# An adaLN transformer block on one core: transfers in the order of need, planned to land later, with a freed residual load and reset stage knobs

## The chip, the core and the metric

The kernel runs on one core of a Trainium2 chip. A core has five engines, each with an instruction queue of its own: PE (TensorE, matmuls into PSUM), DVE (VectorE), ACT (ScalarE), POOL (GpSimd) and SP (SyncE, which here issues nearly all DMA transfers). The engines meet only at semaphores, and each works its instructions strictly in the order in which they were written. The metric is the device time of one execution in microseconds (us).

## The reference

One sequence of 2048 tokens with 640 features, 32 heads of 20, a bilinear gated unit of width 1536, all in bf16:

```
mod = silu(c) @ w_mod                      # six rows of 640: sa, ca, ga, sb, cb, gb
h   = layernorm(x) * (1 + ca) + sa
q, k, v = heads of (h @ wqkv)
p   = softmax(q k^T / sqrt(20))
x   = x + ga * ((p v) @ wo)
h   = layernorm(x) * (1 + cb) + sb
x   = x + gb * (((h @ w_gate) * (h @ w_up)) @ w_down)
```

## The kernel before

**Work and tiles.** The queries are cut into six chunks (512, 512, and four of 256), the heads into eight sets of four. One chunk with one set is an *item*; the very last is split in two, which makes 49. Within an item the scores of 128 keys by the chunk's queries are computed for four heads side by side on PE (line 1494). Two ways lead from scores to exponentials. Most go in groups of two PSUM banks to ACT (816 ACTIVATE instructions of 128x1024, line 1531). A fixed share (QUADS) goes to DVE, which moves them out of PSUM with a shift (line 1555) and builds the power of two from the bits of an int16 (lines 1587, 1595, 1592; a part of the products on POOL, line 1607). Then PE multiplies either kind with the values (line 2154) into the item's accumulator, whose first column is the sum of the softmax.

**Around the attention.** At the start x is loaded, normed and transposed, and Q, K and V are projected. Most of K and Q goes out to DRAM in packed rows and comes back set by set in the layout that the scores need (line 1250 writes from the buffers KPA and KPB, line 1263 loads KT, line 1272 loads QT); the projection of later sets runs beside the scores of earlier ones. At the end of an item DVE transposes the accumulator (T1, line 1686), takes the reciprocal (1691), POOL multiplies (1693), DVE transposes back into OcT (1702), and four or five transfers bring the rows into Ocp (1714). When all eight sets of a chunk are there, the chunk's *suffix* follows beside the scores of the next chunk: load of the residual x (1771) and output projection (944, with evacuation 1793), norm (1810 to 1817, with an addition and a power on POOL, 1813 and 1815), transposes (1855), gate and up (weights loaded by line 1896 into three stg buffers), product into hprod (1928 or 1959), down projection and store (2024, 2033). The last chunk's suffix has nothing beside it. The last two chunks have sets of buffers of their own: for the last but one the residual buffer xckt, and a hprod that lies on the same bytes as xckb, the residual buffer of odd chunks.

**What sets the order.** A planner in the kernel file (class Sched) simulates the engines when the program is built. Each operation is a Task with a duration, a list of tasks it needs, and a priority (a lower number goes first). Whenever an engine is free in the simulation, it takes the first task by priority that is ready by then; `pick_pe` chooses for PE between scores, values and projections with a row of knobs, which STAGE resets from item to item (a missing entry goes back to the default). A transfer is done, in the simulation, when its bytes have passed at DMA_RATE and a latency is over (`finish_issue`, lines 225 to 245); a few early ones have a landing time written by hand. The order that comes out is written into the engines' queues, with a semaphore wait wherever a task needs another. So the plan's times never reach the chip, only its order: if a transfer lands later on the chip than in the plan, the engine that needs it stands, and all that is queued behind it on that engine stands too. Where PE has nothing ready and has been too little busy lately (FILL_MIN), the plan puts a filler, matmuls on the identity without a result (line 2487).

DVE scores of later items ride in the group of an earlier item's scores (`d_attach`), which then waits for the later item's QT and KT as well, if the plan believes them landed.

Of the kernel before, what the change touches and what calls it, by code (L numbers as in the profile page):

```python
# [17 lines left out]
PV_W = 216.0  # L18
# [3 lines left out]
DMA_RATE = 350.0  # L22
# [5 lines left out]
DMA_LAT = 1700.0  # L28
STEAL_END = 66197.894
# [6 lines left out]
class Task:  # L36
    __slots__ = ("head", "hval", "hknow", "eng", "dur", "lat", "deps", "emits", "ctr", "prio", "gate", "acq", "on_start", "slots",
                 "start", "done", "needed", "val", "know", "nleft", "ready", "users", "name", "mode", "seq", "rt", "sem",
                 "nbytes", "cond", "alt", "land", "lk", "dead", "key")

    def __init__(self, eng, dur, emits, deps=(), ctr=None, prio=0.0, lat=None, gate=0, acq=(), on_start=None,
# [25 lines left out]
        self.land = 0.0  # L67
        self.lk = 0
# [58 lines left out]
class Sched:  # L127
# [213 lines left out]
def emit_program(nc, sched, nsem_dma=56):  # L341
# [130 lines left out]
PV_KEEP = 2  # L472
# [62 lines left out]
OPFIRST = 1500  # L535
HT_L = 0.25
# [10 lines left out]
    0: {"LKTOL": 300.0, "D_LATE": 16, "PVMIN": 2, "PVMAX": 14, "PVTOL": 249, "EAGER": 9, "XBACK": 0, "XDPRIO": 1.343, "X_HALF": 0.0, "HOLD": 95, "D_RES": 74, "STEAL_GAP": 200, "PVCAP": 12, "X_LATE": -179.96, "FILL_MIN": 4190.746, "TPRIO": 0.75, "PV_KEEP": 2},  # L547
    1: {"D_LATE": 17, "D_RES": 16, "EAGER": 3},
    2: {"DL": 0.376},
    3: {"PV_KEEP": 3, "HOLD": 128.0},  # L550
    4: {"HOLD": 131.9, "STEAL_GAP": 125.8},
    5: {"PVMAX": 4},
    6: {"PVTOL": 467.4, "X_LATE": -48.0, "D_LATE": 11},
    7: {"DL": 0.501},
    8: {"XBACK": 1},
    9: {"X_HALF": 75.1},
    11: {"DL": 0.443},
    12: {"DL": 0.459, "X_LATE": 52.1, "PVMAX": 4, "HOLD": 102.9},
    13: {"DL": 0.417},
    15: {"D_LATE": 17, "HOLD": 119.5},  # L560
    16: {"EAGER": 3, "X_HALF": 9.1, "HOLD": 111.6},
    19: {"DL": 0.471, "FILL_MIN": 2500, "LKTOL": 78.2},
    20: {"DL": 0.391, "HOLD": 136.1},
    24: {"DL": 0.464},
    25: {"DL": 0.549, "X_LATE": 54.0, "HOLD": 135.1},
    26: {"DL": 0.411, "X_LATE": 24.0, "D_LATE": 14},
    27: {"DL": 0.473, "X_LATE": 150.4, "PVCAP": 10, "HOLD": 149.2},
    29: {"X_HALF": -37.1, "PVMAX": 12, "HOLD": 127.7},
    30: {"X_LATE": -109.9, "HOLD": 140.4},
    31: {"X_HALF": 38.3, "X_LATE": 202.7, "D_RES": 21},  # L570
# [1992 lines left out]
```

## Time and profile before

| | us |
|---|---|
| median of 3 runs | 823.6 (822.26 to 826.3) |
| the profiled execution | 821.17 |
| its span in the profile | 819.4 |
| PE / ACT / DVE / POOL busy | 794.0 / 769.2 / 686.0 / 350.1 |
| granted TensorE clock, mean | 0.995 |

The span reaches from the first to the last instruction of the program; the time of the execution has 1.8 us more around it. The profile's tables by stage give the busy time of an engine in each stretch of the span, then the clock that was granted to TensorE (1.00 is full), the share of the 16 DMA engines in use and the GB/s they moved. The lists of waits say which instruction stood for whom; a wait for several things is put down to the one that came last by the profile, and where the engine named had long been done, it was another, often a transfer. In the list of DMA issues a time is that of the issuing on SP's queue, not of the movement.

### The profile page before, as it was taken

Reading aid. Unit: us, or ns where it says so; the run is one execution under the profiler, and the core shown is the slowest. Engines: PE = TensorE matmul, PEld = TensorE weight load, DVE = VectorE, ACT = ScalarE, POOL = GpSimd, SP = SyncE. Lnnn points to the kernel's source line nnn. Section 1 sums busy time; section 2 is a strip of 40 time slices with the busy share of each in tenths; the row PEclk is TensorE's granted clock in tenths of the full one; section 3 lists DMA queues with packets and bytes.
Section 4 is the critical chain, followed back from the end, with each engine's and each line's share of the span. In section 5 each row is a group of like instructions: output and inputs, shape, how many; then the busy total and the mean of one; then the engine's idle time right before and its main releaser. Section 6 shows DMA issues by size and latency. Waiting matters only on the chain.

```text
span 819.4 us, 34126 instructions
## 1 busy us (share of the span) xinstructions
PE 794.0 (97%) x14871; PEld 346.1 (42%) x14871; DVE 686.0 (84%) x1338; ACT 769.2 (94%) x853; POOL 350.1 (43%) x362
## 2 busy tenths in 40 slices
PE   8999999999989999999999999999999999999998
PEld 4433424332223322233344444444454555434667
DVE  7978887889979899899979878887699989798654
ACT  6899999999989999999999999999999999999931
POOL 3345535474645333244362534533463546035200
PEclk9999999999999999999999999999999999999999
DMA  9743112212340522103100222100441045441420
GB/s 301 233 117 90 49 52 69 58 34 76 99 117 12 155 65 53 45 3 90 35 9 7 56 69 63 36 23 22 96 101 39 26 99 117 107 101 39 97 66 26
DMA packets 136388, 60.49 MB, mean 74 GB/s; under 512 B 100704, under 2 KB 136240, under 8 KB 136240
## 3 DMA queue, kind: packets, MB, share of 16 engines
q1 hardware_dynamic: 135311, 57.16, 27.3%
q8 instruction: 118, 1.93, 1.0%
q10 hardware_dynamic: 928, 1.15, 0.4%
q14 instruction: 31, 0.25, 0.1%
HBM read 46.70 MB, written 8.99 MB: 68 GB/s over the span
## 4 chain that ended last, share of the span: by engine, by line
PE 55%; ACT 26%; DVE 11%; issue 4%; DMA 3%; SPq 1%; POOL 0%; DVEq 0%; ACTq 0%
ACT PP L1531 26%; PE ps_all L1494 18%; PE ps_all L944 18%; PE ps_all L2154 13%; DVE DB L1555 3%; PE ps_all L940 3%; DMA x<-in_A_x_dram 2%; PE ps_all L1204 2%; DVE DSS L1595 1%; DVE DSS L1587 1%; DVE st L1045 1%; DVE DSS L1592 1%; SPq L1714 1%; DMA stg<-in_B_w_up_dram 0%; DVE hT L1109 0%
## 5 line engine op out<-in xcount | busy, mean ns | idle before, releaser
L1531 ACT ACTIVATE PP<-ps_all 128x1024 bf16<-128x1024 f32 x816 | 753.1, 1086 | 10.2 <-PE ps_all L1494 9.4
L1607 POOL TENSOR_TENSOR DSS<-DB,DSS 128x512 bf16<-128x512 bf16 x248 | 281.9, 1158 | 320.0 <-DVE DSS L1595 259.8
L1494 PE MATMUL ps_all<-QT,KT 32*128 32x256 bf16 (+2 forms) x3136 | 321.6, 308 | 12.4 <-ACT PP L1531 9.0
L1555 DVE TENSOR_SCALAR DB<-ps_all 128x512 int16<-128x512 f32 x416 | 277.9, 684 | 60.4 <-PE ps_all L1494 58.4
L1494 PEld LDWEIGHTS ps_all<-QT,KT 32*128 32x128 bf16 x3136 | 89.6, 92 | 239.7 <-ACT PP L1531 183.5
L2154 PE MATMUL ps_all<-PP,Vf 128*32 128x256 bf16 (+2 forms) x2520 | 166.9, 311 | 0.0
L944 PE MATMUL ps_all<-h2T,stg 128*32 128x256 bf16 (+2 forms) x2260 | 124.7, 306 | 1.7 <-DMA stg<-in_B_w_up_dram 1.2
L2154 PE MATMUL ps_all<-DSS,Vf 128*32 128x256 bf16 (+1 forms) x1232 | 85.6, 315 | 0.5 <-DVE DSS L1592 0.3
L2154 PEld LDWEIGHTS ps_all<-PP,Vf 128*32 128x32 bf16 (+1 forms) x2520 | 49.8, 94 | 82.1 <-issue 76.4
L1595 DVE TENSOR_SCALAR DSS<-DB 128x2048 int16<-128x2048 int16 x104 | 74.1, 713 | 0.0
L1587 DVE TENSOR_SCALAR DSS<-DB 128x2048 int16<-128x2048 int16 x104 | 71.3, 685 | 0.3
L1693 POOL TENSOR_TENSOR OTn<-OT,invT 128x256 bf16<-128x256 f32 (+1 forms) x47 | 39.0, 830 | 66.1 <-DVE invT L1691 65.8
L944 PEld LDWEIGHTS ps_all<-h2T,stg 128*32 128x32 bf16 x2260 | 52.1, 96 | 30.2 <-issue 19.2
L944 PE MATMUL ps_all<-wd,hprod 128*32 128x320 bf16 (+1 forms) x1328 | 61.6, 283 | 0.0
L1592 DVE TENSOR_TENSOR DSS<-DB,DSS 128x2048 bf16<-128x2048 bf16 x42 | 52.5, 1251 | 0.2
L2154 PEld LDWEIGHTS ps_all<-DSS,Vf 128*32 128x32 bf16 (+1 forms) x1232 | 29.6, 95 | 21.8 <-issue 11.7
L944 PE MATMUL ps_all<-wV,hT 128*32 128x160 bf16 x1280 | 37.2, 234 | 0.4
L944 PEld LDWEIGHTS ps_all<-wd,hprod 128*32 128x32 bf16 x1328 | 30.0, 96 | 16.0 <-issue 10.4
L944 PE MATMUL ps_all<-wo,Ocp 128*32 128x320 bf16 (+1 forms) x692 | 30.5, 278 | 4.1 <-DMA Ocp<-OcT 3.0
L1686 DVE STREAM_TRANSPOSE OT<-ps_all 128x256 f32<-128x256 f32 (+2 forms) x49 | 25.7, 525 | 10.1 <-PE ps_all L2154 9.9
L1204 PE MATMUL ps_all<-hT,wk 128*32 128x512 bf16 (+1 forms) x360 | 31.8, 382 | 0.2
L1204 PE MATMUL ps_all<-hT,wq 128*32 128x512 bf16 x375 | 31.6, 382 | 0.1
(132 smaller groups left out, 526.7 us busy)
## 6 DMA issues: line engine op xcount, KB each, us to landing
stg<-in_B_w_gate_dram SPq DMA_DIRECT2D x62, 160.0 KB
stg<-in_B_w_up_dram SPq DMA_DIRECT2D x62, 160.0 KB
KT<-k_rows SPq DMA_DIRECT2D x112, 32.0 KB
wm<-in_w_mod_dram SPq DMA_DIRECT2D x3, 800.0 KB
x<-in_A_x_dram SPq DMA_DIRECT2D x7, 320.0 KB
k_rows<-KPA SPq DMA_DIRECT2D x16, 128.0 KB
QT<-q_rows SPq DMA_DIRECT2D x32, 64.0 KB
wd<-in_B_w_down_dram SPq DMA_DIRECT2D x1, 1920.0 KB
```

Source lines behind the costliest of these rows:

```text
L944: return lambda e, b: e.matmul(ps[32 * x:32 * x + 32, b, c0 + o:c0 + o + w], lhs()[:, 32 * x:32 * x + 32], rhs() if w == n else rhs()[:, o ...
L1204: f = [lambda e, b_, k=k, x=x: e.matmul(ps[x:x + min(32, w - x), b_, :], wx[:, k, r0 + x:r0 + min(x + 32, w)], hT[tc][:, k, :], tile_posit ...
L1494: ems.append(lambda e, i=i, kt=kt: e.matmul(dstf()[:, i * u.n:(i + 1) * u.n], KT[32 * u.s:32 * u.s + 32, u.j, kt * 128:(kt + 1) * 128], QT ...
L1531: return e.activation(PPs[g % 2][:, cellp["p"], 0:nu * 512], ps[:, b0:b0 + nu, :].rearrange("p b c -> p (b c)"), AFT.Exp, scale=ESCALE)
L1555: return e.tensor_scalar(DBl[st_["slot"]][:, x * 512:(x + 1) * 512], bank(cell["b"]), EBIAS, 0.0, op0=ALU.add, op1=ALU.max)
L1587: return e.tensor_scalar(DSl[st_["ss"][0]][:, :], DBl[st_["slot"]][:, :], 0x7F, 0x3F00, op0=ALU.bitwise_and, op1=ALU.bitwise_or)
L1592: return e.tensor_tensor(d, DBl[st_["slot"]][:, :].bitcast(BF16), d, ALU.mult)
L1595: return e.tensor_scalar(DSl[st_["ss"][1]][:, :], DBl[st_["slot"]][:, :], 0x7F80, 2, op0=ALU.bitwise_and, op1=ALU.bitwise_or)
L1607: return e.tensor_tensor(d, DBl[st_["slot"]][:, x * w:x * w + w].bitcast(BF16), d, ALU.mult)
L1686: t1 = Task("dve", n * 1.1 + 70, lambda e: e.transpose(OT[:, 0:n], ps[:, item_info[it]["bank"], 0:n].rearrange("p (b q r) -> p b r q", q=3 ...
L1693: f3 = lambda e: e.tensor_tensor(OTn[:, 0:n].rearrange("p (b c r) -> p b r c", c=32, r=2), OT[:, 0:n].rearrange("p (b r c) -> p b r c", c= ...
L2154: ems.append(lambda e, i=i, kt=kt, stt=stt, stp=stp: e.matmul(ps[32 * s:32 * s + mc, bk, 0:u.n], Vf[:, (kt * H + 4 * u.j + s) * VW:(kt * H ...
```

## The change

Five things are changed. (1) The planner's model: transfers after 25 us move at 240 GB/s instead of 350, and those issued after 60 us land 1000 ns later, unless marked `firm`; some matmul costs go up by 1 to 3 ns. (2) The priorities of transfers on SP's queue: writes of K and early Q rows, loads of KT and QT by set and chunk, and the pieces of Ocp of the last two sets. (3) In the suffix of the last but one chunk the residual load, the norm's output and the transposes no longer wait for the stores of xckb; hprod's writers do (`hp_free`). (4) At the end of a chunk the reciprocal and the second transpose have priority 0.4 instead of 1.5 on DVE, and the addition and power of the norm -1 instead of 1 on POOL. (5) The STAGE table is reset; its entry for item 0 and the DL values stay.

```diff
-PV_W = 216.0
+PV_W = 219.0
...
+DMA_RATE_2 = 240.0
+DMA_MARGIN = 1000.0
+DMA_M0 = 60000.0
...
-            self.dma_free = b + task.nbytes / DMA_RATE
-            task.done = task.land or self.dma_free + (DMA_LAT_2 if early else DMA_LAT + DMA_SLOW * task.nbytes)
+            self.dma_free = b + task.nbytes / (DMA_RATE if early or task.firm else DMA_RATE_2)
+            task.done = task.land or self.dma_free + (DMA_LAT_2 if early else DMA_LAT + DMA_SLOW * task.nbytes +
+                                                      (0.0 if task.firm or start < DMA_M0 else DMA_MARGIN))
...
+ENDP, END3, P_POW = 0.4, 0, -1.0
...
 STAGE = {
...
-    1: {"D_LATE": 17, "D_RES": 16, "EAGER": 3},
-    2: {"DL": 0.376},
-    3: {"PV_KEEP": 3, "HOLD": 128.0},
...
+    1: {"FILL_MIN": 4712.6, "PV_KEEP": 2, "LKTOL": 200.7},
+    2: {"DL": 0.376, "PVMAX": 4},
+    3: {"HOLD": 124.6},
...
-    43: {"HOLD": 179.1},
-    44: {"PV_KEEP": 1, "X_LATE": 6.7, "HOLD": 113.2},
-    45: {"HOLD": 117.9},
+    42: {"HOLD": 47.1, "XBACK": 0},
+    45: {"EAGER": 9, "PVTOL": 185.1},
 }
...
-    C512, C320, C128, C1 = 216.0, 136.0, 57.0, 26.0
+    C512, C320, C128, C1 = 219.0, 137.0, 57.0, 26.0
...
-        return max(n / 2.4 + 3.0, 60.0)
+        return max(n / 2.4 + 6.0, 60.0)
...
-                dst(), buf[p0:p0 + n_, cell["t"].slots["kp"], :]), [te], prio=1.5, dur=450.0)
+                dst(), buf[p0:p0 + n_, cell["t"].slots["kp"], :]), [te], prio=1.5 if late_q else 1.0, dur=480.0)
...
-                        dps, prio=1.4, dur=450.0) for s in range(4)]
+                        dps, prio=1.1 + .01 * (j + tc / 4), dur=480.0) for s in range(4)]
...
-                            [...], prio=1.6, dur=450.0)]
+                            [...], prio=1.11 + .01 * (j + NSET * ci), dur=480.0)]
...
+        pe_ = ENDP if j == NSET - 1 and ci < NC - 1 else 1.5
...
-                                            OT[:, 0:n].rearrange("p (b c) -> p b c", c=32)[:, :, 0:1]), [t1], prio=1.5)
+                                            OT[:, 0:n].rearrange("p (b c) -> p b c", c=32)[:, :, 0:1]), [t1], prio=pe_)
...
-            t = dma("sp", nr * n * 2, f, dps, prio=2, dur=720.0)
+            t = dma("sp", nr * n * 2, f, dps, prio=1.05 if j >= NSET - 2 else 2, dur=720.0)
+            t.firm = ci == NC - 1 and it >= len(items) - 2
...
-            first = list(sfx_done["qd1"]) + outs_r[1] if ci == NC - 2 else bd["tr"] + bd["h2T"] + bd["hp"] + outs_r[0]
+            first = list(sfx_done["qd1"]) if ci == NC - 2 else bd["tr"] + bd["h2T"] + bd["hp"] + outs_r[0]
+        hp_free = first + (outs_r[1] if ci == NC - 2 else [])
...
-            p1 = dve(75, f1, [ag], prio=LN2T if tail else LN2P) if tail else pool(220, f1, [ag], prio=1)
+            p1 = dve(75, f1, [ag], prio=LN2T if tail else LN2P) if tail else pool(220, f1, [ag], prio=P_POW)
...
-                      [p1], prio=1)
+                      [p1], prio=P_POW)
...
-                    return [eg, dve(ps_cost(n), f, [r.last, eg] + (first if alt else bd.get("hp", []) + proj_early + kv_last), prio=1)]
+                    return [eg, dve(ps_cost(n), f, [r.last, eg] + (hp_free if alt else bd.get("hp", []) + proj_early + kv_last), prio=1)]
```

More of the change, by code (lines that the diff above doesn't have):

```diff
@@ L67, in __init__ @@
         self.land = 0.0
+        self.firm = False
         self.lk = 0
@@ L568 @@
[L568 to L578 removed]
+    25: {"DL": 0.549},
@@ new lines @@
+    26: {"DL": 0.411, "X_LATE": 65.8, "PVMAX": 3, "EAGER": 8},
+    27: {"DL": 0.473},
+    29: {"HOLD": 38.5, "PVMIN": 2, "LKTOL": 11.4},
+    30: {"D_RES": 7, "PVMAX": 4, "X_HALF": -29.6},
+    31: {"X_LATE": -186.8, "X_HALF": 32.8, "HOLD": 130.6},
+    32: {"EAGER": 5, "D_LATE": 14, "HOLD": 153.7, "LKTOL": 269.4},
+    33: {"DL": 0.442, "XBACK": 4, "PV_KEEP": 1},
+    34: {"X_LATE": 5.0},
+    35: {"X_LATE": 15.7},
+    36: {"DL": 0.524, "EAGER": 3},
+    38: {"HOLD": 43.6},
+    42: {"HOLD": 47.1, "XBACK": 0},
@@ L1273, in packed_round @@
                             QT[ci][:, j, :], QS[1024 * tc + 128 * j:1024 * tc + 128 * j + 128, so:so + n]),
-                            [x for l in done for x in l] + q_zero[tc] + (x0_done if ci else []), prio=1.6, dur=450.0)]
+                            [x for l in done for x in l] + q_zero[tc] + (x0_done if ci else []), prio=1.11 + .01 * (j + NSET * ci), dur=480.0)]
             if tc not in LATEQ:
@@ L1697, in item_end_tasks @@
         direct = j == NSET - 1 and ci == NC - 1
-        if T3_POOL and not direct:
+        if T3_POOL and not direct and not (END3 and j == NSET - 1):
             t3 = pool(n * 2.2 + 200, f3, [t2], prio=0)
         else:
-            t3 = dvl(sb_cost(n, 1.04), f3, [t2], prio=1.5)
+            t3 = dvl(sb_cost(n, 1.04), f3, [t2], prio=pe_)
         t4 = dve(n * .55 + 65, lambda e: e.transpose(OcT[:, cell["s"], 0:n].bitcast(F32), OTn[:, 0:n].bitcast(F32)), [t3],
-                 prio=1.5)
+                 prio=pe_)
         pcs = [] if direct else oc_pieces(j)
```

40 lines of the change are left out of this document (17 added, 23 removed).

## The prediction

> **What bounds the kernel now.** I read the page first (busy shares, costliest groups), then the table by stage for the exponentials alone, then the waits of those stages in which that table shows a hole, then the chain and the DMA queue around each hole.
>
> ```profile
> PE 794.0 (97%) x14871; PEld 346.1 (42%) x14871; DVE 686.0 (84%) x1338; ACT 769.2 (94%) x853; POOL 350.1 (43%) x362
> L1531 ACT ACTIVATE PP<-ps_all 128x1024 bf16<-128x1024 f32 x816 | 753.1, 1086 | 10.2 <-PE ps_all L1494 9.4
> ```
>
> ACT carries 816 exponentials, 753.1 us of its 769.2, and stood idle before them for only 10.2 us in the whole run. PE shows 97%, but a busy PE is partly one that is paced by the exponentials. Which of the two sets the time is read by stage (columns: length, ACT busy with the exponentials and their count, granted clock, DMA share, GB/s):
>
> ```profile
> 80.00:100.00 20.00, 18.39 (x21) 1.00 0.22 55
> 200.00:220.00 20.00, 20.00 (x23) 1.00 0.36 103
> 220.00:240.00 20.00, 18.48 (x20) 1.00 0.46 119
> 240.00:260.00 20.00, 17.46 (x19) 0.91 0.14 36
> 580.00:600.00 20.00, 18.37 (x20) 0.91 0.55 120
> 720.00:740.00 20.00, 19.39 (x22) 1.00 0.29 66
> 780.00:800.00 20.00, 4.09 (x5) 1.00 0.23 57
> ```
>
> 200 to 220 is a stage as most are: 20.00 of 20. So from about 40 us to 784 us ACT is the pacer, and four places lose time: 1.61 us at 80-100, 1.52 + 2.54 at 220-260, 1.63 at 580-600, 0.61 at 720-740, together 7.91 us. From 784 on ACT is nearly empty and PE alone runs the rest of the last two chunks. What held ACT in the four places (one line each, in that order: us in total, times, longest), and what held PE, whose order is fixed:
>
> ```profile
> ACT PP L1531 <- PE ps_all L1494: 1.3, 1, 1.3
> ...
> ACT PP L1531 <- PE ps_all L1494: 3.9, 3, 2.7
> ...
> ACT PP L1531 <- PE ps_all L1494: 1.5, 3, 0.5
> ...
> ACT PP L1531 <- PE ps_all L1494: 0.6, 1, 0.6
> ```
>
> ```profile
> PE ps_all L944 <- DMA Ocp<-OcT: 3.0, 1, 3.0
> ...
> PE ps_all L944 <- DMA stg<-in_B_w_up_dram: 1.2, 1, 1.2
> PE ps_all L944 <- DMA xckt<-in_A_x_dram: 1.0, 1, 1.0
> ```
>
> ACT waited for scores, 1.3 + 3.9 + 1.5 + 0.6 = **7.3 us**, and three of the four times PE stood before a matmul whose transfer hadn't landed, with the scores queued behind it. The fourth PE wait, at 88 us, is put down to ACT, which had ended long before; the DMA queue and PE show the transfer behind it:
>
> ```profile
> 85.67 1.30 SPq L1272 DMA_DIRECT2D QT<-q_rows  x2
> ...
> 89.24 0.39 PE L1494 MATMUL ps_all<-QT,KT 32*128 32x512 bf16 x3 [1.52 <-ACT PP L1531]
> ```
>
> Two loads of QT were issued until 86.97, and 2.3 us later PE's 1.52 us of waiting end with a score that reads QT. I take it for that landing; a score of a later set rides in that group.
>
> **The change part by part.** Its weight is a planner's belief, so few instructions change: the exponentials, the share of DVE and every matmul stay, only their order and that of the transfers moves.
>
> *Later landings.* The plan now lets a transfer issued after 60 us land 1000 ns later and move at 240 instead of 350 GB/s. A matmul in the planned order is put where its transfer is believed landed, so PE goes on with scores and values in between. These are the issue-to-landing rows of the chain for three of the four:
>
> ```profile
> 238.47 1.96 DMA Ocp<-OcT
> ...
> 581.01 3.93 DMA stg<-in_B_w_up_dram
> ...
> 721.71 3.32 DMA xckt<-in_A_x_dram
> ```
>
> PE missed them by 3.0, 1.2 and 1.0 us (and QT by 1.5). The added 1.0 us, and the lower rate (320 KB take 1.37 instead of 0.94 us, and several transfers stand in line at each place), cover the last two and nearly QT, the first only together with the new order. What PE does meanwhile: the waiting work is projection, not scores, and none of it is needed at once. Value: the four ACT waits go, **-7.3 us**; ends 0 (each wait comes back in another place) and -7.9 (the whole of the four holes).
>
> *Transfers by need.* The pieces of Ocp of the last two sets go from priority 2 to 1.05, ahead of QT (1.6 before, now 1.11 and up by set and chunk), and the writes of K and early Q from 1.5 to 1.0. The queue ahead of the 3.0 us wait, where three of the first chunk's last four pieces had gone:
>
> ```profile
> 235.30 1.26 SPq L1250 DMA_DIRECT2D q_rows<-KPB  x2
> 236.67 1.76 SPq L1272 DMA_DIRECT2D QT<-q_rows  x4
> 238.47 0.76 SPq L1714 DMA_DIRECT2D Ocp<-OcT  x1
> ```
>
> The fourth waited behind 1.26 + 1.76 = 3.0 us of writes and of loads that only later chunks need. With the new order it leaves at 235.3, 3 us earlier, which is the wait: the same 3 us as above, not a second gain. What becomes late instead is late Q: each of its writes (still 1.5) now stands behind a group of four QT loads, 1.76 us, and holds one of two KPB slots meanwhile; its readers are the four short chunks, in the later half of the run. I take 0, with ends 0 and +3 us (two such groups, while a PSUM bank is held).
>
> *Residual of the last but one chunk.* Its load no longer waits for the stores of the buffer beside it; the first writer of that place, hprod, takes the wait over. The queue at the end of that chunk, and the out projection that the load releases:
>
> ```profile
> 701.16 7.06 SPq L1714 DMA_DIRECT2D Ocp<-OcT  x8
> ...
> 715.34 0.52 SPq L2033 DMA_DIRECT2D out_dram<-xckb  x1
> ...
> 717.84 3.77 SPq L1714 DMA_DIRECT2D Ocp<-OcT  x5
> 721.71 0.42 SPq L1771 DMA_DIRECT2D xckt<-in_A_x_dram  x1
> ```
>
> ```profile
> 725.08 0.66 PE L944 MATMUL ps_all<-wo,Ocp 128*32 128x320 bf16 x16 [0.97 <-DMA xckt<-in_A_x_dram]
> ```
>
> A set sends 4, 5, 4, 5, 5, 4, 5, 4 pieces (its 80 rows against tiles of 128), so the run of 8 is the chunk's last set and the next chunk's first, and the 5 are the next chunk's second. The chunk's own last piece is thus the fourth of eight, out by 701.16 + 7.06/2 = 704.7 and landed near 706.7 (1.96 us as above). The load stood behind the store of 715.34 and five pieces that it has nothing to do with, and landed at 721.71 + 3.32 = 725.03. Freed, its gate is 20 groups before the last chunk's first scores, far ahead of 700. So the out projection may start at 707 and not at 725, **18 us earlier**. What is that worth? PE alone in these stages (its busy time is the second column), and the fillers in them (matmuls on the identity, of no result):
>
> ```profile
> 700.00:720.00 20.00, 19.70 (x428) 8.94 (x422) 16.93 (x30) 20.00 (x23) 1.24 (x2) 1.00 0.47 113
> 720.00:740.00 20.00, 18.04 (x364) 7.63 (x360) 18.05 (x37) 19.39 (x22) 6.83 (x8) 1.00 0.29 66
> 740.00:760.00 20.00, 19.76 (x454) 10.01 (x454) 16.62 (x36) 20.00 (x23) 12.27 (x12) 1.00 0.19 44
> ```
>
> ```profile
> 700.00:720.00 20.00, 2.03 (x24) 0.46 (x24) 1.00 0.47 113
> 720.00:740.00 20.00, 3.04 (x36) 0.69 (x36) 1.00 0.29 66
> 740.00:784.00 44.00, 0.40 (x4) 0.10 (x4) 1.00 0.37 81
> ```
>
> In 40 us PE spent 0.30 + 1.96 idle and 2.03 + 3.04 on fillers, 7.3 us, of which 1.0 is the wait counted above: 6.3 us in which it had no projection to do. After 740 there is next to none left to fill; work that is done before 740 shortens what follows the last exponential. I take **-4.0 us**, two thirds of the 6.3, since the norm between out projection and gate still has its own length and PE must find the work ready; ends 0 (the work is stopped by the norm or by the bank it needs) and -6.3. Hprod's new wait costs nothing here: the store leaves at 715.9, and the first product comes behind the whole projection and the norm.
>
> *Accumulators and power first.* At a chunk's end the reciprocal and the second transpose go ahead of the DVE evacuations, and POOL takes the power before products. One jumped evacuation or product is about 1 us of a chain that lies within the 6.3 us above; I take nothing more for it. If the cover is gone, it costs or gives that 1 us.
>
> *Costs and stage table.* Matmuls are believed 1 to 3 ns longer, and the knobs of some thirty of the 49 sets are reset. No instruction is added. The L1531 row bounds the gain: 10.2 - 7.3 = 2.9 us of idle elsewhere. On the other side new planned waits can come: I take **+1.6 us**, one hole as that at 80-100, by which the plan believes scores late that are not; ends -2.9 and the rival's +20 below. The marking as punctual in the diff touches nothing: it is set for pieces of the last two sets, which send none.
>
> *Sum.* -7.3 - 4.0 + 1.6 = -9.7 us. The profiled execution took 821.17 us (span 819.4 and 1.8 around it), so 811.5 on its scale. The median of the runs shown, 823.6, lies 2.4 higher, so **813.9 us** by that.
>
> [...]
>
> ```profile
> 241.29 2.15 ACT L1531 ACTIVATE PP<-ps_all 128x1024 bf16<-128x1024 f32 x2 [2.75 <-PE ps_all L1494]
> 243.91 1.02 ACT L1531 ACTIVATE PP<-ps_all 128x1024 bf16<-128x1024 f32 x1 [0.47 <-PE ps_all L1494]
> 245.61 1.94 ACT L1531 ACTIVATE PP<-ps_all 128x1024 bf16<-128x1024 f32 x2 [0.68 <-PE ps_all L1494]
> ```
>
> After the wait of 2.75 us come two of 0.47 and 0.68 with PE working, and at 580-600 all three are at most 0.5: I count these as the wait's own follow-up, from a slower PE. [...]
>
> **The rivals.**
>
> *All of it comes.* Holes of 7.9 go, the tail gives 6.3, no new wait: -14.2, 809.4 us. For it: PE has fillers to spare, so planning late costs it nothing. Against: some of the fillers stand between the steps of the norm, which an earlier start moves but doesn't shorten.
>
> *The waits only change place.* The DMA queue issues without a pause around 235 to 239, each issue taking 0.4 to 0.8 us of it; whatever goes first, something goes last. If PE then waits for QT, stg or q_rows in the same places, two thirds of 7.3 stay, -2.4; if the out projection finds no room beside the chunk before it, which PE is still finishing, the tail gives 1.5; with the new wait of 1.6 that is -2.3, 821.3 us. For it: the queue is as long as before. Against: what goes last now is needed much later.
> [...]
>
> *Slower: K is believed late.* K goes through DRAM: written, waited for, loaded, and no score of a quarter set can be put ahead of its load.
>
> ```profile
> SPq L1263 <- DMA k_rows<-KPA: 10.3, 10, 1.4
> ```
>
> The loads already waited ten times for the write's landing. Two legs, each believed 1.0 us later and 0.1 slower, are 2.2 us. Place: the first chunk past 60 us, some 20 quarter sets. Where the plan has less than 2.2 us in hand it now leaves ACT without a score that is in truth ready. With 1.2 us in hand that is 1.0 each, +20 us, against -11.3: +8.7, 832.3 us. It decides from 0.77 us each, that is under 1.4 us in hand, on: 15.4 - 11.3 is the 4.1 us of a measurable loss. Against it: a waiting PE can take the next projection earlier, which brings K forward, and K's writes and loads move up in the queue.
>
> **How the numbers follow.** Forecast 0.54 (811 to 817.5 on the median's scale), all of it 0.16, changed place 0.19, slower 0.11. The range reaches from 808.5, just under the full gain, to 822.0, over the case of changed place; the slower case and some strays are left out. A measurement of this kernel tells about 0.5% (4.1 us) from no change: faster, under 819.5, is the first two and a sliver of the third, 0.72; within it 0.17; slower, over 827.7, 0.11.
>
> **What would show it.** Right: the exponentials' table reads near 20.00 at all four places, PE's waits for DMA are under 1 us in sum, the clock is 1.00 throughout, and the last exponential ends about 6 to 7 us earlier. The tail's part is right if the load of xckt is issued before 700, its out projection starts well before 720, the fillers after 700 shrink from 5 us to under 2, and some 31 us instead of 35 follow the last exponential. Wrong: a hole of exponentials between 60 and 200 us with PE waiting for nothing (K believed late), PE waits for q_rows, QT or stg of the old size elsewhere, or a tail as long as before, with PE idle in it (the last chunk's own chain).

## The result, and the profile after

| | us | against the kernel before | |
|---|---|---|---|
| the changed kernel, 4 executions | 813.62 (812.5 to 814.7) | 823.86 | ratio 0.987 [0.984, 0.990] |
| the same once more, 6 executions | 810.27 (808.33 to 816.9) | 822.66 | ratio 0.986 [0.982, 0.989] |

The forecast was 813.9 us and 0.988. The first profile of the changed kernel has a span of 812.9 us, the second one of 808.2 (before: 819.4). Both are needed: they have the same order of instructions and differ by where the clock fell. First the exponentials by stage in the first profile (columns as in the prediction: length, ACT busy and count, granted clock, DMA share, GB/s), then the only wait that PE's list puts down to a transfer, and one that it puts down to nothing:

```profile
80.00:100.00 20.00, 19.65 (x22) 1.00 0.30 74
200.00:220.00 20.00, 19.46 (x22) 1.00 0.30 88
220.00:240.00 20.00, 20.00 (x23) 1.00 0.47 118
240.00:260.00 20.00, 20.00 (x23) 1.00 0.11 31
260.00:280.00 20.00, 15.54 (x17) 0.66 0.06 16
580.00:600.00 20.00, 20.00 (x23) 1.00 0.48 105
720.00:740.00 20.00, 19.88 (x23) 1.00 0.65 149
```

```profile
PE ps_all L973 <- DMA wm<-in_w_mod_dram: 0.6, 1, 0.6
```

```profile
88.81 0.40 PE L1502 MATMUL ps_all<-QT,KT 32*128 32x512 bf16 x4 [0.71 <-issue]
```

The four places of the prediction read 19.65, 20.00 twice, 20.00 and 19.88; the waits for Ocp, stg and xckt are gone. (What PE waits for at L973 is a load of the first microseconds.) The wait at 88 us is the one that the prediction took for QT: two loads of QT leave until 87.40 here, so by the same reading it has shrunk from 1.52 to 0.71 us; the second profile has none. In place of the four holes stands one new one, 4.46 us at 260 to 280, under a clock of 0.66. The second profile doesn't have it, but has one of its own, 1.84 us at 60 to 80 under a clock of 0.91 (19.48 in the first):

```profile
60.00:80.00 20.00, 18.16 (x21) 0.91 0.33 89
...
200.00:220.00 20.00, 19.46 (x22) 1.00 0.29 87
...
260.00:280.00 20.00, 20.00 (x23) 1.00 0.31 97
```

The tail in the first profile: the freed load, its first out projection, and the fillers from 700 on (all there are).

```profile
664.45 0.53 SPq L1782 DMA_DIRECT2D xckt<-in_A_x_dram  x1
...
702.37 0.53 PE L952 MATMUL ps_all<-wo,Ocp 128*32 128x320 bf16 x12
```

```profile
700.00:720.00 20.00, 0.00 (x0) 1.00 0.08 19
720.00:740.00 20.00, 0.62 (x8) 1.00 0.65 149
740.00:780.00 40.00, 1.20 (x12) 1.00 0.35 79
```

The load leaves at 664.45 where it left at 721.71, the out projection starts at 702.37 where it started at 725.08, and the fillers shrink from 5.5 us to 1.8.

**Where the time came from.** The costliest group of the page, first profile and then second, and the last exponentials of the second profile:

```profile
L1539 ACT ACTIVATE PP<-ps_all 128x1024 bf16<-128x1024 f32 x816 | 751.0, 1157 | 7.4 <-PE ps_all L1502 6.5
```

```profile
L1539 ACT ACTIVATE PP<-ps_all 128x1024 bf16<-128x1024 f32 x816 | 750.2, 1160 | 3.9 <-PE ps_all L1502 3.1
```

```profile
766.73 8.65 ACT L1539 ACTIVATE PP<-ps_all 128x1024 bf16<-128x1024 f32 x9
```

Against before's row (753.1 busy, 10.2 idle) the second profile has 6.3 us less idle time ahead of the exponentials and 2.9 us less busy time for the same 816. I take these 2.9 us for the restarts: after a wait the next exponential stands alone (1.02 us in the rows of the prediction, where 20 us without a hole hold 22 to 23, one each 0.9 us), so a wait would cost a little more than its idle time. Together 9.2 us; the last exponential ends at 775.38 instead of 784.09, 8.7 us earlier. What follows it takes 32.8 us instead of 35.3. 8.7 + 2.5 is the 11.2 us between the two spans.

### The profile page after: what moved, and what is told of

Its sections match the earlier page's. It is cut to its first block, busy times and chain, and to the rows that moved or that the text cites. A ratio compares the mean times of both kernels' runs of the same rounds, so it can differ in the third digit from the quotient of the medians.

```text
span 812.9 us, 34131 instructions
## 1 busy us (share of the span) xinstructions
PE 796.0 (98%) x14867; PEld 345.3 (42%) x14867; DVE 685.9 (84%) x1337; ACT 767.0 (94%) x851; POOL 360.6 (44%) x374
## 4 chain that ended last, share of the span: by engine, by line
PE 49%; ACT 40%; issue 6%; DVE 3%; DMA 1%; SPq 0%; ACTq 0%; DVEq 0%
ACT PP L1539 40%; PE ps_all L1502 17%; PE ps_all L952 13%; PE ps_all L2165 11%; PE ps_all L1212 3%; PE ps_all L948 3%; DMA wm<-in_w_mod_dram 1%; DVE DB L1563 1%; PE ps_all L1109 1%; DVE DSS L1595 1%; PE ps_all L1866 1%; PE ps_all L1148 1%; DVE DSS L1603 0%; PE ps_all L2498 0%; DVE KPA L1221 0%
## 5 line engine op out<-in xcount | busy, mean ns | idle before, releaser
L1615 POOL TENSOR_TENSOR DSS<-DB,DSS 128x512 bf16<-128x512 bf16 x260 | 295.5, 1155 | 325.1 <-DVE DSS L1603 273.4
L952 PE MATMUL ps_all<-h2T,stg 128*32 128x256 bf16 (+2 forms) x2272 | 122.8, 303 | 0.2 <-DVE DB L1563 0.2
L1600 DVE TENSOR_TENSOR DSS<-DB,DSS 128x2048 bf16<-128x2048 bf16 x39 | 49.3, 1265 | 0.1
L1212 PE MATMUL ps_all<-hT,wk 128*32 128x512 bf16 (+1 forms) x360 | 32.8, 382 | 0.2 <-DVE Vf L1301 0.2
L952 PE MATMUL ps_all<-wo,Ocp 128*32 128x320 bf16 (+1 forms) x664 | 30.7, 280 | 0.3
```

The lines of the kernel that those rows point to most:

```text
L952: return lambda e, b: e.matmul(ps[32 * x:32 * x + 32, b, c0 + o:c0 + o + w], lhs()[:, 32 * x:32 * x + 32], rhs() if w == n else rhs()[:, o ...
L1212: f = [lambda e, b_, k=k, x=x: e.matmul(ps[x:x + min(32, w - x), b_, :], wx[:, k, r0 + x:r0 + min(x + 32, w)], hT[tc][:, k, :], tile_posit ...
L1600: return e.tensor_tensor(d, DBl[st_["slot"]][:, :].bitcast(BF16), d, ALU.mult)
L1615: return e.tensor_tensor(d, DBl[st_["slot"]][:, x * w:x * w + w].bitcast(BF16), d, ALU.mult)
```

## The experiments

Each ratio is against executions of the kernel before on the same chip. The planner simulates the whole kernel, so most single parts of the change reorder everything. Where that was to be kept out, the order of the kernel before was frozen: the plan is made as before, and then one transfer is moved in SP's queue. The later landings alone, the accumulators alone and the changed kernel without its priorities or with its old knobs could not be run: for these the simulation comes to no complete order. So no run shows what the later landings do by themselves. The marking as punctual is settled without a run: with it and without it, the instructions of all five engines stand in the same order.

**One piece of Ocp ahead, nothing else** (order of before, frozen; the piece is the last of the first chunk's last set, put right behind the one before it; `ahead` moves its first task in SP's queue to right behind its second).

```diff
+    moved = [t for t in sc.order["sp"] if t.name == "OCP0.7"]
+    ahead(sc, moved[-1], moved[-2])
```

> The kernel before in its own order, with one transfer moved: the first chunk's last piece of Ocp goes out right behind the third, ahead of two writes of Q rows and four loads of QT. If the gain of the change is that PE no longer stands for transfers: PE's wait of 3.0 us for Ocp is gone, the 4.06 us of holes of the exponentials at 220 to 260 us fall below 0.8, the granted clock there is 1.00 instead of 0.91, and the time falls by 3.4 to 4 us (ratio 0.995 to 0.996). If waits only change place (rival): PE stands for QT, stg or q_rows instead, holes over 2 us stay, and the time is within 1.5 us of before. If the gain is that of the newly planned order as a whole (second theory): under 1 us.

Measured 819.43 us, ratio 0.9958 [0.9936, 0.9981], which is 3.5 us. Its exponentials:

```profile
80.00:100.00 20.00, 17.08 (x18) 0.91 0.34 88
220.00:240.00 20.00, 19.94 (x22) 1.00 0.50 130
240.00:260.00 20.00, 20.00 (x23) 1.00 0.21 59
```

The holes of 1.52 and 2.54 us are gone with the wait of 3.0, and so is the low clock of 240 to 260; the place at 80 to 100, which wasn't touched, stays, and is 1.3 us deeper in this execution, at a clock of 0.91.

**The freed residual alone** (part 3 of the change on the kernel before).

```diff
-            first = list(sfx_done["qd1"]) + outs_r[1] if ci == NC - 2 else bd["tr"] + bd["h2T"] + bd["hp"] + outs_r[0]
+            first = list(sfx_done["qd1"]) if ci == NC - 2 else bd["tr"] + bd["h2T"] + bd["hp"] + outs_r[0]
+        hp_free = first + (outs_r[1] if ci == NC - 2 else [])
...
-                    return [eg, dve(ps_cost(n), f, [r.last, eg] + (first if alt else bd.get("hp", []) + proj_early + kv_last), prio=1)]
+                    return [eg, dve(ps_cost(n), f, [r.last, eg] + (hp_free if alt else bd.get("hp", []) + proj_early + kv_last), prio=1)]
```

> The kernel before with the freed residual load alone; the plan is the same until the end of the last but one chunk. By my sum: the load of xckt is issued before 700 us, the out projection behind it starts before 712 instead of 725, the hole of 0.61 us at 720 to 740 goes, fillers after 700 fall from 5 us to under 2, some 31 us instead of 35.3 follow the last exponential, and the time falls by 4 to 5 us (ratio 0.994 to 0.995). If the tail is bound by the last chunk's own chain (rival): 34 us or more follow the last exponential, PE is idle in them, and the time falls by under 1 us.

Measured 817.95 us, ratio 0.9941 [0.9916, 0.9966], 4.9 us, with a tail of 30.7 us. To see what the tail consists of, I counted which matmuls of the last but one chunk run behind the last exponential: gate and up (they read h2Tt), then down (hprodt); columns: stretch and length, PE busy with them (and how many), clock, DMA. Before, then this kernel:

```profile
784.09:819.40 35.31, 2.73 (x80) 0.99 0.10 30
...
784.09:819.40 35.31, 6.89 (x192) 0.99 0.10 30
```

```profile
785.77:816.50 30.73, 0.00 (x0) 1.00 0.07 23
...
785.77:816.50 30.73, 4.49 (x116) 1.00 0.07 23
```

The last chunk's own work is the same in both. 80 + 76 matmuls fewer, 5.1 us of PE, make the 4.6 us by which the tail is shorter.

**Three transfers alone**: that piece, the freed residual, and the residual of the chunk before it, moved behind the three pairs of stg loads that it stood ahead of.

```diff
+    named = {t.name: t for t in sc.order["sp"]}
+    ahead(sc, named["XC3"], named["W2.5.1"])
```

> The kernel before with three transfers treated: the piece of Ocp moved as in the run before, the residual load of the fourth chunk moved behind the three pairs of weight loads that it stood ahead of at 579 us, and the freed residual of the last but one chunk. Everything else is the old plan. If the gain is these transfers: 4.0 + 1.6 + 4.5, some 10 us less, ratio 0.987 to 0.989, as the whole change (0.9873). If the newly planned order carries the gain: less than half of that, ratio over 0.994.

Measured 812.87 us, ratio 0.9889 [0.9857, 0.9922]. The two ratios above multiply to 0.990. So the old landing times, knobs and priorities with two or three transfers moved by hand come, within the intervals, to the whole change. ("Two or three", since the hole at 580 to 600 that the third was to close is absent without it too, as shown below.)

**The changed kernel with the residual waiting for the stores again.**

```diff
-            first = list(sfx_done["qd1"]) if ci == NC - 2 else bd["tr"] + bd["h2T"] + bd["hp"] + outs_r[0]
-        hp_free = first + (outs_r[1] if ci == NC - 2 else [])
+            first = list(sfx_done["qd1"]) + outs_r[1] if ci == NC - 2 else bd["tr"] + bd["h2T"] + bd["hp"] + outs_r[0]
+        hp_free = first
```

> The changed kernel with the residual load waiting for the stores again. By my sum 4 us come back (ratio to before 0.992), all of it after 700 us: the out projection of the last but one chunk starts after 720, fillers grow, the tail is 35 us or more. More than 4 us, if the later landings that are now planned add to the wait, since store, load and projection then stand in line with 1 us more for each. If the residual is worth nothing beside the new plan (rival): within 1 us of the changed kernel, ratio 0.986 to 0.989.

Measured 824.13 us, ratio 1.0002 [0.9972, 1.0031]: the whole gain is given back. PE's list has no wait for a transfer behind the start in this kernel, and its exponentials stand idle for 2.7 us only. Of the 13.9 us between its span and that of the second profile 10.6 are in the tail: the load, and the same two counts.

```profile
726.55 0.41 SPq L1782 DMA_DIRECT2D xckt<-in_A_x_dram  x1
```

```profile
778.70:822.10 43.40, 7.62 (x240) 1.00 0.24 59
...
778.70:822.10 43.40, 6.70 (x192) 1.00 0.24 59
```

The load leaves 5 us later than before, 240 gate and up matmuls are left instead of 80, and the tail is 43.4 us. For comparison the second profile of the changed kernel:

```profile
775.39:808.20 32.81, 0.00 (x0) 1.00 0.07 22
...
775.39:808.20 32.81, 7.26 (x192) 1.00 0.07 22
```

In the changed kernel one load is worth 10.6 us of tail, though alone it was worth 4.6. I expected 4 or more; how much it is was a surprise. Why this plan leaves so much more than the one before when the load is late was not taken apart.

**The priorities of the transfers alone** (part 2 on the kernel before, with the issues believed 30 ns longer as in the change).

```diff
-                dst(), buf[p0:p0 + n_, cell["t"].slots["kp"], :]), [te], prio=1.5, dur=450.0)
+                dst(), buf[p0:p0 + n_, cell["t"].slots["kp"], :]), [te], prio=1.5 if late_q else 1.0, dur=480.0)
...
-                        dps, prio=1.4, dur=450.0) for s in range(4)]
+                        dps, prio=1.1 + .01 * (j + tc / 4), dur=480.0) for s in range(4)]
...
-            t = dma("sp", nr * n * 2, f, dps, prio=2, dur=720.0)
+            t = dma("sp", nr * n * 2, f, dps, prio=1.05 if j >= NSET - 2 else 2, dur=720.0)
```

> The kernel before with the priorities of its transfers alone changed (writes of K and early Q rows, loads of KT and QT, the last two sets' pieces of Ocp), planned with the old landing, the residual still waiting for the stores and the old knobs. Theory from the single moved piece: the wait for Ocp at 238 us goes and the holes at 220 to 260 with it, ratio 0.995 to 0.997; QT at 88 us and the load of xckt at 721 stay. Rival, priced in the prediction at 0 to +3 us: a load that now goes later (QT, stg, late Q) is waited for instead, ratio 0.999 to 1.003. The tail stays at 35 us by both.

Measured 821.83 us, ratio 0.9993 [0.9971, 1.0015]: no gain, which is the rival. At 220 to 260 the holes are nearly gone (19.13 and 20.00), but:

```profile
80.00:100.00 20.00, 14.24 (x16) 0.83 0.26 67
```

```profile
87.14 0.84 SPq L1272 DMA_DIRECT2D QT<-q_rows  x2
...
89.29 0.39 PE L1494 MATMUL ps_all<-QT,KT 32*128 32x512 bf16 x3 [3.34 <-issue]
```

Two loads of QT are issued at 87.14, where they were at 85.67. Loads of K go first, so the write of Q rows that QT reads leaves at 83.16 instead of 82.17, and SP's queue stands 1.3 us for its landing ahead of the loads, where it stood 0.5. The next score waits 3.34 us instead of 1.52 (I take it for the landing of QT, as in the prediction). What goes first makes something else go last.

**The new STAGE table alone**, and **the table with the freed residual** (parts 5, and 5 with 3, on the kernel before; the second has the residual's edit as above).

```diff
-    1: {"D_LATE": 17, "D_RES": 16, "EAGER": 3},
-    2: {"DL": 0.376},
...
+    1: {"FILL_MIN": 4712.6, "PV_KEEP": 2, "LKTOL": 200.7},
+    2: {"DL": 0.376, "PVMAX": 4},
...
```

> The kernel before with the new STAGE table alone, the rest old. Theory: the table was made for the other transfer model and brings nothing by itself; the waits for transfers stay of the old size at the same or other places, ratio 0.998 to 1.006. Rival: the knobs carry a part of the gain (PE kept busier where it was least so, hence fewer dips of the clock), ratio under 0.996. The tail stays at 35 us by both.

> The kernel before with two parts of the change: the new STAGE table and the freed residual; old transfer priorities, old landing. Theory A: the gain has two halves that any plan can give, PE not standing before the last piece of Ocp at 238 us and the tail's earlier work; the ratios of the table alone and of the residual alone multiply, 0.9952 x 0.9941 = 0.989, and the tail is 31 to 33 us. Theory B: without the later landings the waits only move; ratio over 0.992, with PE waits for transfers over 1 us in sum in its profile.

Measured 819.69 us, 0.9952 [0.9931, 0.9973], and 819.80 us, 0.9948 [0.9924, 0.9971]. The table brings 3.9 us by itself, against my expectation. In its profile PE has no wait for Ocp, and 200 to 280 us is without a hole, but two other stages have one:

```profile
200.00:280.00 80.00, 80.00 (x88) 1.00 0.35 100
...
80.00:100.00 20.00, 16.70 (x19) 1.00 0.30 78
620.00:640.00 20.00, 17.68 (x20) 0.83 0.09 21
```

The first is the hole that the one moved piece closes too. The residual on top brings nothing that can be told from zero. That is against theory A; the ratio is the one that theory B gave, but not for its reason, since behind the start PE's list has one wait for a transfer, of 0.4 us. The residual is loaded early (667.8), and the tail is 36.3 us as with the table alone:

```profile
782.59:818.90 36.31, 1.46 (x40) 1.00 0.08 25
...
782.59:818.90 36.31, 6.89 (x192) 1.00 0.08 25
```

This plan has the load and doesn't use it: the out projections' first evacuation is at 715.1 and the norm's two results come at 724.4 and 735.1 (in the kernel with the residual alone 713.8, 721.0 and 727.2), and the down projection is left whole.

**The changed kernel again, with scores doubled, and with lean fillers.** These three ask about the fallen clock. Unaltered; then with the score matmuls of eleven groups (255 to 272 us) issued twice; then with each filler cut to one of its four matmuls.

```diff
+    for t in sc.order["pe"]:
+        if t.name in {f"S{g}" for g in range(252, 263)}:
+            n = t.head or len(t.emits)
+            t.emits = t.emits[:n] + t.emits
```

```diff
+        if t.name == "fill":
+            t.emits = t.emits[:1]
```

> The changed kernel once more, unaltered, for a second profile and more times. Question: the halved clock at 262.7 to 276.3 us in the first profile (260 to 280: 15.54 of 20.00 us of exponentials, clock 0.66), which cost 5.4 us. Theory A, it belongs to this plan: the place shows again, the executions lie at 812.5 to 814.7 as before, ratio 0.986 to 0.988. Theory B, it comes and goes from one execution to the next, as the clock at 440 to 452 did in two of three kernels with the same order there: some executions have a higher mean clock and lie near 808 to 810, and the time falls by some 1 to 1.6 us for each 0.002 of mean clock. In the new profile each dip stands at one of the stretches in which PE is least busy (88, 201, 219, 263 us).

> The changed kernel in its own order, with the score matmuls of eleven groups around 255 to 272 us issued twice (same operands, same result), so that PE is never short of work in the stretch in which the clock fell. Theory: the clock falls where PE is only partly busy over a few us, without a single long idle; then 260 to 280 reads 20.00 at clock 1.00 and the median is 2 to 5 us under that of the unaltered kernel beside it, ratio to before 0.981 to 0.985. Rival: the dip has nothing to do with PE's load there; then it appears as often as in the unaltered kernel, or elsewhere, and the doubled matmuls cost 0 to 2 us more, ratio 0.987 to 0.990.

> The changed kernel in its own order with each filler cut from four matmuls to one (11.8 us of PE become about 3; no result depends on them). Theory: the clock follows PE's load over a few us, and the fillers hold it up; then the clock falls at 400 to 460 us, where most of them stand, in most executions, mean clock 0.995 or lower, ratio 0.988 to 0.996. Rival: only a longer idle stretch brings the clock down; no pause grows over 1 us here, so clock and time stay as in the unaltered kernel, ratio 0.984 to 0.987.

| executions (us at mean clock) | |
|---|---|
| unaltered, ratio 0.9856 [0.9818, 0.9894] | 808.33 at 1.000; 809.96, 810.07, 810.47 at 0.998; 813.32 at 0.994; 816.90 at 0.987 |
| scores doubled, 0.9841 [0.9810, 0.9872] | 809.34, 809.44, 809.55, 809.76, 810.55 at 1.000; 813.01 at 0.996 |
| lean fillers, 0.9859 [0.9826, 0.9893] | 808.48 at 1.000; 809.89, 810.80 at 0.998; 813.92, 814.23 at 0.994; 815.81 at 0.990 |
| before, 23 beside the first two | 819.68 at 0.998; median 822.66; 829.18 at 0.981 |

Within a kernel the time follows the mean clock: 8.6 us for 0.013 in the unaltered changed kernel, 9.5 us for 0.017 in the one before, about 0.6 us for each 0.001. The fall at 263 us comes and goes: theory B of the first expectation. Its last sign failed: the second profile's own dip, in the stage of 60 to 80 us (clock 0.91), is at none of the four places named. With the scores doubled five of six executions kept the full clock, where one of ten of the unaltered kernel did (its four first executions lie at 0.991 to 0.994). Against that one the doubled scores cost 1.0 us or more, so the medians (809.65 and 810.27) can't be told apart; I had expected 2 to 5 us. 260 to 280 reads 19.79 in its profile, at a clock of 1.00. Cutting the fillers to a quarter, for which I had the same theory, shows no change: three of six executions have a mean clock of 0.994 or less, where I had expected most, and two of six of the unaltered kernel do. So these runs by themselves leave open what brings the clock down; the last section takes it up from the rows.

**Accumulators late** in the changed kernel: thirteen more reciprocals ahead of the real one at five chunk ends.

```diff
+    pad = alloc("pad", [128, 13, 16], F32)
...
+        if pe_ == ENDP:
+            t2.name = "RECIP"
+            t2.slots["pad"] = [lambda e, x=x: e.reciprocal(
+                pad[:, x, 0:nb32].unsqueeze(2), OT[:, 0:n].rearrange("p (b c) -> p b c", c=32)[:, :, 0:1]) for x in range(13)]
...
+    for t in sc.order["dve"]:
+        if t.name == "RECIP":
+            t.emits = t.slots["pad"] + t.emits
```

> The changed kernel with thirteen more reciprocals of the accumulator (into a scratch tile, some 2.6 us of DVE) ahead of the real one at the end of each of the first five chunks, which takes back most of what reading the accumulators first gains there: from the end of the first transpose to that of the second it is 3.6, 2.9, 1.6, 2.2 and 1.8 us in the changed kernel and 12.0, 9.5, 5.5, 5.8 and 5.1 in the one before. Theory of the prediction: this chain is covered, so the median stays within 1.5 us of the unaltered kernel, ratio 0.984 to 0.988. Rival: the out projections are planned so close behind that PE stands for Ocp at each chunk's end, 1 to 2.6 us each, 5 to 13 in all, ratio 0.992 to 1.001, with PE waits for Ocp in the profile.

Measured 812.94 us, 0.9875 [0.9840, 0.9910], beside 810.27 and 0.9856 for the unaltered kernel in another series, the intervals widely overlapping; 2.7 us, where I had allowed 1.5. In its profile PE waits for no piece of Ocp; the span is 810.0 at clock 1.000 against 808.2 at 0.998, so 1.8 us or a little more. 1.0 us of it are holes at 200 to 240, where the unaltered kernel reads 19.46 and 20.00:

```profile
200.00:220.00 20.00, 19.35 (x21) 1.00 0.30 86
220.00:240.00 20.00, 19.12 (x21) 1.00 0.48 121
```

```profile
220.43 0.39 PE L1503 MATMUL ps_all<-QT,KT 32*128 32x512 bf16 x3 [1.61 <-DVE DB L1564]
```

The second hole is not the chain's: PE stands for scores that DVE moves out of PSUM behind the added reciprocals. And the edit did less than was meant. The thirteen take 1.1 to 1.6 us and not 2.6, and from the end of the first transpose to that of the second it is now 5.0, 3.6, 2.2, 3.1 and 2.5 us: 0.6 to 1.4 us are taken back at each end, of the 3.3 to 8.4 that the change gains there. So the run shows a delay of that size to be covered, not the whole chain. At the first end the rows speak against the whole: in the second profile the four pieces are out at 221.47 + 3.53 = 225.0 and the first out projection starts at 231.1; 8.4 us later they would be out at 233.4 (an estimate from these rows).

## Why the prediction was right

**"The four ACT waits go, -7.3 us."** The waits go, and they were worth about their length. Idle time ahead of the exponentials fell by 6.3 us in the second profile, and busy time by 2.9 more. That PE's stand for Ocp was worth its length is shown by the one moved piece (3.5 [1.6, 5.3] us for a wait of 3.0). That it is the later landings that remove the waits, as the prediction has it, is not shown: under the old landings the new table alone removes the wait for Ocp, and the priorities alone shorten it to 1.1 us. One of the four places was worth less than the profile made it: at 580 to 600 the kernel with the residual alone, with the same order on PE up to that point, has a wait for stg of 0.3 instead of 1.2 us and no hole. A wait in one execution's profile needn't be in the median.

```profile
560.00:600.00 40.00, 40.00 (x45) 1.00 0.31 74
```

**"Transfers by need ... the same 3 us."** The place was right, and the cost of it, "I take 0", was wrong for the priorities by themselves: they make QT late at 89 us and give all of it back. I had looked for lateness in late Q, in the short chunks; it came in the first chunk, at a load next to the one that had been missed already. In the full change the place at 80 to 100 is nearly filled (19.65 and 20.00), so another part of it mends that; which, was not separated.

**"Freed residual, -4.0 us."** The mechanism was right: earlier out projection (702.4; forecast 707), fewer fillers (1.8 us; forecast under 2), less work behind the last exponential. By itself it gave 4.9 [2.8, 6.9] us and the 31 us of tail that I had forecast. In the full change the tail shrinks by 2.5 only, since 192 down matmuls are left there instead of 116, and yet taking the residual away costs all. The step that failed is that it could be priced as one term: it is worth 4.9 us on the old plan, nothing that can be told from zero on the old plan with new knobs, and 11 to 12 us in the full change (ratio 1.0002 against 0.9873 and 0.9856).

**"Costs and stage table, +1.6 us."** Failed in sign. No set stood for K that was believed late: from 40 to 200 us the exponentials stood for 1.75 us in the first profile and 2.72 in the second, before 2.29. One small hole did come, 0.54 us at 200 to 220 in both profiles. But the table alone makes the kernel 3.9 us faster; I take that for the wait for Ocp that is gone from its profile, less what the holes at 80 to 100 and 620 to 640 take back. It overlaps with the first term, so the two can't be added: I had priced knobs as noise around a fixed set of waits, when each new plan rolls anew which transfers are met too early.

**"Accumulators and power first ... nothing more."** Not settled. The jump was mis-sized: I put it at 1 us. At the first chunk's end the second transpose comes at 220.61 instead of 229.11:

```profile
216.78 0.72 DVE L1686 STREAM_TRANSPOSE OT<-ps_all 128x512 f32<-128x512 f32 x1 [0.19 <-PE ps_all L2154]
...
229.11 0.43 DVE L1702 STREAM_TRANSPOSE OcT<-OTn 128x256 f32<-128x256 f32 x1
```

```profile
216.78 0.70 DVE L1695 STREAM_TRANSPOSE OT<-ps_all 128x512 f32<-128x512 f32 x1
...
220.61 0.43 DVE L1711 STREAM_TRANSPOSE OcT<-OTn 128x256 f32<-128x256 f32 x1
```

That is 8.5 us earlier. The moved piece shows that the hole behind this end can be closed without it. Whether the changed plan could do without it no run shows: the late accumulators took back a small part only, and by the estimate given there the first end could not.

**The rivals.** "All of it comes" (809.4) is where the second series lies (810.27). "The waits only change place" is what the priorities do alone. "K is believed late" didn't happen.

**What would show it.** All signs came but three: the clock wasn't 1.00 throughout in either profile, the tail is 32.8, not 31, and the last exponential is not 6 to 7 us earlier. (PE's waits for transfers are 0.6 us in sum by the list, but 1.3 with the wait at 88 us.) In the second profile it is 8.7 us earlier, in the first only 4.0 (766.81 + 13.23 = 780.04), so 4.7 us later than in the second, which I take for the clock's fall; the profiled pair alone, 821.17 and 814.7, would have read as two thirds of the forecast.

```profile
766.81 13.23 ACT L1539 ACTIVATE PP<-ps_all 128x1024 bf16<-128x1024 f32 x14
```

**The sum.** That it came out is partly luck, because errors met: the table's term had the wrong sign, the tail came out 1.5 us smaller, and the steadier clock added. The first series lies 0.3 us from the forecast and the second 3.6 us under it. In the series of the second profile the median clock is 0.998, before 0.994; at 0.6 us for 0.001 that is 2.4 of 12.4 us. At like clock, 0.998, the changed kernel took 810.0 to 810.5 in three executions and the kernel before 819.7 in one: 9.2 to 9.7 us, which is the forecast's 9.7.

## What to carry to other kernels

Where engines work in a fixed order, look for the single transfer before which the pacing engine's supplier stands, and move that one: one piece of Ocp gave 3.5 us, while a general rule of priority gave nothing, because it made another load late. A load that is freed pays only if the plan puts work on it, so count the work that is left behind the pacer's last instruction rather than look at the load. Take a second profile before a hole is explained: two of the holes here, one before and one after the change, weren't there in another execution with the same order on PE.

## What the runs showed of the hardware that was not expected

**The clock falls with PE at work.** In the first profile of the changed kernel:

```profile
250.00:260.00 10.00, 10.00 (x101) 3.07 (x100) 9.77 (x18) 10.00 (x13) 2.69 (x4) 1.00 0.21 60
...
265.00:270.00 5.00, 5.00 (x35) 1.08 (x27) 2.50 (x4) 2.99 (x4) 1.15 (x1) 0.50 0.02 4
270.00:275.00 5.00, 5.00 (x37) 1.00 (x40) 3.23 (x6) 3.53 (x4) 2.26 (x2) 0.50 0.06 16
```

```profile
262.97 0.60 PE L1502 MATMUL ps_all<-QT,KT 32*128 32x512 bf16 x2 [0.37 <-ACT PP L1539]
```

(The first five pairs of numbers of the upper rows are PE, its weight loads, DVE, ACT and POOL.) From about 263.0 to 276.6 the clock reads 0.50; the longest pause of PE in the 10 us ahead is 0.37 us. It is not a matter of the program alone: the second profile of the same program has the clock at 1.00 there. So too at 440 us: the kernel before and the kernel with the residual alone have the same order on PE up to there and the same pauses, and only the second lost its clock (for each: PE's two pauses, then PE in the stage).

```profile
439.59 0.39 PE L1494 MATMUL ps_all<-QT,KT 32*128 32x256 bf16 x4 [0.35 <-ACT PP L1531]
440.51 0.39 PE L1494 MATMUL ps_all<-QT,KT 32*128 32x256 bf16 x4 [0.53 <-ACT PP L1531]
```

```profile
440.00:460.00 20.00, 19.32 (x356) 1.00 0.11 27
```

```profile
439.89 0.39 PE L1494 MATMUL ps_all<-QT,KT 32*128 32x256 bf16 x4 [0.36 <-ACT PP L1531]
440.81 0.39 PE L1494 MATMUL ps_all<-QT,KT 32*128 32x256 bf16 x4 [0.53 <-ACT PP L1531]
```

```profile
440.00:460.00 20.00, 19.47 (x276) 0.74 0.10 23
```

In the other direction a pause of 1.10 us at 202 us in the second profile of the changed kernel cost no clock (1.00 in its stage of 200 to 220). The prediction put the short waits behind the long one at 241 us down to a slower PE and took them for the wait's own follow-up. For the 3.0 us wait that holds: with the piece moved, the clock stays at 1.00 there. But the low clocks of before are not those of its two longest waits: the wait of 1.52 us at 88 us is longer than the 1.2 us at 585 and cost no clock in that profile, while with the piece moved nearly the same wait, 1.54 us, is followed by a fall.

So as a general account it doesn't hold that the length of a wait decides: the clock falls with pauses of 0.37 and 0.53 us just ahead, and stays at 1.00 over 1.10 and 1.52. What is regular is the times. In the kernel before the clock is low from 241.95 to 245.36 and from 586.69 to 590.10, 3.41 us each; the two starts lie 344.74 us apart, which is 101 times 3.413; and the fall in the first profile of the changed kernel lasts 13.65 us, four times as long.

**What two of the traces say of the cause.** This is an estimate from the rows of the kernel before and of the first profile of the changed one. Count each matmul by its columns, at 0.21 us for 512 (rows of four, eight and twelve projection matmuls of 128*32 with 512 columns take 0.39, 0.61 and 0.83 us, so about 0.22 more for each four side by side), times the share that its stationary operand has of the largest in the rows, 128*128 (a quarter for the 32*128 of a score matmul), spread over its time in the trace. Add this up over stretches of 3.41 us on the grid on which the clock changes in that profile. Between 30 and 775 us the stretches right ahead of the three falls in these two traces have 0.92 and 1.12 us (before) and 1.17 (after), and the other 427 stretches at full clock have 1.27 or more. The grid lies differently over the program in the two executions (the falls at 241.95 and 262.98 are 6.16 steps of it apart), and so the same work can fall on either side: around 440 us the two stretches of the grid have 1.52 and 1.47 in the kernel before, which kept its clock, but one laid from 438.45 to 441.86 has 1.12. There the clock fell with the residual alone (at about 442.16, by a mean clock of 0.54 from 442 to 444; the same rows stand 0.30 us later in that profile). So too little work in one stretch of 3.41 us, not a long pause, fits these four falls; for the falls of the other profiles it is not shown, and no run was made to test it.
